# Attention weights turned unmasked and undivided, and the scaling moved behind the product with V

## Chip, cores and metric

The kernel runs on one core of one Trainium2 chip. The metric is the device time of one execution in microseconds. The kernel before takes 677.22 us, the median of three runs (677.18 to 677.5).

## The reference

An attention with a sliding window and four sink keys, followed by a feed-forward layer with a leaky maximum, all in float32:

```python
scores = (q @ k.T) / sqrt(D)                       # B,H,S,D = 4,8,768,64
keep = (pos[None] < 4) | ((rel >= 0) & (rel < 128))
scores = where(keep, scores, -1e9)
a = exp(scores - max(scores))
a = a / (sum(a) + 1e-9)
x = (a @ v), heads side by side                    # 3072 x 512
h = x @ w_in                                       # 512 -> 2048
out = (maximum(h, 0) + alpha * minimum(h, 0)) @ w_out
```

## The kernel before

The 3072 rows of x are 12 chunks of 256 queries (c; three chunks per batch, CPB). A chunk's feed-forward part is 16 slots (f, blocks of 128 of the 2048 columns). A slot is twelve matmuls of 128x256 for the first layer (L894: the high half of x by both halves of w_in, the low half by the high one), then ScalarE's multiplication by alpha (L898), VectorE's maximum (L899), ScalarE's rounded copy `gh` (L900) and VectorE's rest `gl` (L901), and, two slots later (LAG), six matmuls of 128x512 of the second layer (L931, L932, L929). First-layer results alternate between two PSUM banks.

While the matmuls of chunk c run, the attention of chunk c+1 is put between them, spread over twelve of the sixteen slots. Chunks 0 to 2 go other ways, which the change leaves alone. For chunks 3 to 11 (PAIRED) a head (h) and a half of its queries (u) is one step:

- SyncE (SP) loads `stage` (L443), VectorE and ScalarE split it into `kq` (L561 to L565).
- TensorE: two score matmuls of 128x260 (L597, L598): 256 window keys and 4 sinks.
- VectorE adds the mask and takes the row's extreme in one custom operation (L610), ScalarE takes the exponential with its sum (L614), both in a tile `pt_`. Masked weights come out as zeros.
- Then the head is finished. VectorE adds 1e-9 to the sums and takes reciprocals (L643, L644). A query's window covers at most the 128 keys before its block and the 128 of its own, and their two triangles don't overlap; so one custom operation (L655; L651 where a batch begins) adds the two blocks and divides, into `comb`. GpSimd divides the sink weights (L659).
- After two heads: VectorE turns 32x32 blocks of the pair's 512 columns (L741), SP writes the tile to DRAM (`swap`, L744) and reads it back in another order (L746), which makes it a full transpose. VectorE multiplies by two triangular masks to part the blocks again (L770 for pairs 0 and 1 into `wa`; L757 and L759 for pairs 2 and 3).
- The sinks of all heads are split, turned and sent through DRAM alike (L689, L690, L697, SP's `turns` L699 and `sinkT` L701).
- TensorE: four matmuls for the sinks (L859), and later 48 for the values (L786 for pairs 0 and 1, L875 for 2 and 3), 64 columns wide, two heads side by side. ScalarE and VectorE split the result into `xh` (L881) and `xl` (L882), the input of the next chunk's first layer.

The order is set ahead of time. Each operation is given to a planner (`Plan`) with its engine, an estimated cost, what it reads and writes, and for a DMA its bytes; the planner draws one queue for each engine, in which instructions then run strictly in order, and gives out the few buffers of each kind in turn. SP's DMAs go through one such queue too. What an instruction waits for can therefore hold all that stands behind it on its engine.

## Time and profile before

| | |
|---|---|
| time, median of three runs | 677.22 us (677.18 to 677.5) |
| span of the profiled execution | 676.2 us |
| TensorE busy | 663.8 us, 98% |
| VectorE busy | 525.8 us, 78% |
| ScalarE busy | 397.5 us, 59% |
| GpSimd busy | 34.5 us, 5% |
| bytes moved by DMAs | 85.19 MB |

The profile shows one execution; its span is 1.0 us under the median of the measured times. A row of a group reads: line, engine, operation, out<-in, shapes, count | busy us in all, mean ns of one | idle us ahead of them and what ended it. A row of the timeline reads: start in us, length, engine, line, operation. The length of a matmul includes the way through the array, so the pace is read from the distance of starts. Rows of waits read: us in total, times, the longest.

### The profile page before, as it was taken

Reading aid. Unit: us, or ns where it says so; the run is one execution under the profiler, and the core shown is the slowest. Engines: PE = TensorE matmul, PEld = TensorE weight load, DVE = VectorE, ACT = ScalarE, POOL = GpSimd, SP = SyncE. Lnnn points to the kernel's source line nnn. Section 1 sums busy time; section 2 is a strip of 40 time slices with the busy share of each in tenths; the row PEclk is TensorE's granted clock in tenths of the full one; section 3 lists DMA queues with packets and bytes.
Section 4 is the critical chain, followed back from the end, with each engine's and each line's share of the span. In section 5 each row is a group of like instructions: output and inputs, shape, how many; then the busy total and the mean of one; then the engine's idle time right before and its main releaser. Section 6 shows DMA issues by size and latency. Waiting matters only on the chain.

```text
span 676.2 us, 13243 instructions
## 1 busy us (share of the span) xinstructions
PE 663.8 (98%) x4532; PEld 580.5 (86%) x4534; DVE 525.8 (78%) x1750; ACT 397.5 (59%) x1066; POOL 34.5 (5%) x115
## 2 busy tenths in 40 slices
PE   9989999999999999999999999999999999999996
PEld 4577898888989989989988988988998988998995
DVE  6999999968967976986986995995895994994331
ACT  6989888827636726736636735644744753853332
POOL 2110000001000000000000000010000000000000
PEclk9979999999999999999999999999999999999999
DMA  8684641424343453443443433552542543420001
GB/s 314 229 277 151 241 187 39 127 71 147 122 133 107 122 148 93 145 132 95 141 118 114 143 107 93 163 140 61 172 128 78 161 128 88 142 94 17 32 2 35
DMA packets 58683, 85.19 MB, mean 126 GB/s; under 512 B 9072, under 2 KB 35056, under 8 KB 58608
## 3 DMA queue, kind: packets, MB, share of 16 engines
q1 hardware_dynamic: 55056, 71.17, 34.7%
q10 hardware_dynamic: 3552, 13.11, 5.4%
q8 instruction: 37, 0.61, 0.4%
q14 instruction: 38, 0.31, 0.1%
HBM read 67.22 MB, written 17.04 MB: 125 GB/s over the span
## 4 chain that ended last, share of the span: by engine, by line
PE 83%; DVE 9%; ACT 5%; issue 2%; POOL 0%; DMA 0%; ACTq 0%; SPq 0%; POOLq 0%
PE bank L894 35%; PE bank L931 12%; PE bank L932 11%; PE bank L929 11%; PE bank L786 3%; PE bank L598 3%; PE bank L597 3%; PE bank L875 2%; DVE wa L396 2%; ACT pt L614 1%; ACT wa L382 1%; DVE wa L394 1%; DVE w L404 1%; DVE g L899 1%; DVE gl L901 1%
## 5 line engine op out<-in xcount | busy, mean ns | idle before, releaser
L894 PE MATMUL bank<-xh,w 128*128 128x256 f32 x1536 | 307.9, 283 | 0.4 <-DVE g L899 0.2
L894 PEld LDWEIGHTS bank<-xh,w 128*128 128x128 f32 x1536 | 250.6, 189 | 9.0 <-DVE g L899 3.0
L894 PE MATMUL bank<-xl,w 128*128 128x256 f32 x768 | 215.1, 280 | 0.1
L898 ACT ACTIVATE g<-bank,param 128x256 f32<-128x256 f32 x192 | 90.5, 472 | 117.4 <-PE bank L894 113.1
L931 PE MATMUL bank<-w,gh 128*128 128x512 f32 x382 | 151.7, 397 | 0.2 <-ACT gh L900 0.2
L932 PE MATMUL bank<-w,gh 128*128 128x512 f32 x382 | 150.1, 393 | 0.0
L894 PEld LDWEIGHTS bank<-xl,w 128*128 128x128 f32 x768 | 145.2, 189 | 4.4 <-DVE xl L808 0.3
L614 ACT ACTIVATE pt<-pt,nm 128x260 f32<-128x260 f32 (+1 forms) x192 | 94.5, 493 | 53.5 <-DVE nm L610 53.1
L899 DVE TENSOR_TENSOR g<-bank,g 128x256 f32<-128x256 f32 x192 | 79.7, 419 | 51.4 <-ACT g L898 50.9
L929 PE MATMUL bank<-w,gl 128*128 128x512 f32 x382 | 119.5, 394 | 0.0
L900 ACT CAST gh<-g 128x256 fp32r<-128x256 f32 x192 | 76.9, 404 | 59.7 <-DVE g L899 59.6
L901 DVE TENSOR_TENSOR gl<-g,gh 128x256 fp32r<-128x256 f32 x192 | 80.5, 423 | 26.5 <-ACT gh L900 23.0
L610 DVE CUSTOM_DVE_ANT_0 pt<-bank,masks 128x260 f32<-128x260 f32 (+1 forms) x192 | 75.0, 401 | 19.3 <-PE bank L598 15.5
L929 PEld LDWEIGHTS bank<-w,gl 128*128 128x128 f32 x382 | 70.7, 188 | 16.2 <-issue 0.7
L931 PEld LDWEIGHTS bank<-w,gh 128*128 128x128 f32 x382 | 71.9, 188 | 9.5 <-ACT gh L900 0.7
L932 PEld LDWEIGHTS bank<-w,gh 128*128 128x128 f32 x382 | 71.9, 188 | 8.3
L563 DVE TENSOR_TENSOR kq<-stage,kq 64x392 fp32r<-64x392 f32 x80 | 45.3, 566 | 2.7
L659 POOL TENSOR_TENSOR sink<-pt,ri 128x8 f32<-128x8 f32 x80 | 20.8, 264 | 504.7 <-DVE ri L644 358.8
L597 PE MATMUL bank<-kq 128*128 128x260 f32 (+1 forms) x160 | 44.4, 278 | 1.3 <-DVE nm L610 1.3
L598 PE MATMUL bank<-kq 128*128 128x260 f32 (+1 forms) x160 | 45.0, 281 | 0.0
L655 DVE CUSTOM_DVE_ANT_0 comb<-pt,ri 128x128 f32<-128x128 f32 x136 | 43.1, 343 | 0.4
L561 ACT CAST kq<-stage 128x392 fp32r<-128x392 f32 x80 | 40.9, 512 | 0.7 <-ACT pt L614 0.2
(130 smaller groups left out, 686.9 us busy)
## 6 DMA issues: line engine op xcount, KB each, us to landing
stage<-qk SPq DMA_DIRECT2D x80, 324.0 KB, 2.9
wraw<-w ACTq DMA_DIRECT2D x12, 1024.0 KB, 5.9
swap<-comb SPq DMA_DIRECT2D x36, 256.0 KB, 2.0
comb<-swap SPq DMA_DIRECT2D x36, 256.0 KB, 3.2
v<-vq SPq DMA_DIRECT2D x36, 192.0 KB, 2.5
out_dram<-ob SPq DMA_DIRECT2D x22, 256.0 KB, 3.5
wraw<-w SPq DMA_DIRECT2D x4, 1024.0 KB, 12.0
v<-vp SPq DMA_DIRECT2D x8, 192.0 KB, 6.9
```

The source lines that it names most:

```text
L597: nc.tensor.matmul(s[:, w0], qh()[:, qs], ks()[:, kw], start=True, stop=False)
L598: nc.tensor.matmul(s[:, w0], ql()[:, qs], ks()[:, kw], start=False, stop=True)
L610: op("DVE", dve(n), lambda: nc.vector.tensor_tensor_reduce(out=pt.at[:, u, w0], in0=s.at[:, w0], in1=masks[:, i, w0], scale=-0.125, scalar ...
L614: op("ACT", exp(n), lambda: nc.scalar.activation(pt.at[:, u, w0], pt.at[:, u, w0], AF.Exp, bias=nm.at[:, h, u:u + 1], scale=-1.0, accum_ou ...
L894: nc.tensor.matmul(h(), fin.at[:, 0, part, ks], rhs.at[:, kt], start=(kt == 0 and n == 0), stop=(kt == KT - 1 and n == 2))
L898: op("ACT", act(QC, True), lambda: nc.scalar.activation(g.at, h(), AF.Copy, scale=alt[:, f:f + 1]), reads=[bk, known("param")], writes=[g])
L899: op("DVE", dve(QC), lambda: nc.vector.tensor_tensor(g.at, h(), g.at, ALU.max), reads=[bk], writes=[g])
L900: op("ACT", cast(QC), lambda: nc.scalar.copy(gh.at, g.at), reads=[g], writes=[gh])
L901: op("DVE", dve(QC), lambda: nc.vector.tensor_tensor(gl.at, g.at, gh.at.bitcast(F32), ALU.subtract), reads=[g, gh], writes=[gl])
L929: nc.tensor.matmul(o2[j].at, gl.at[:, js], fin.at[:, 1, 0], start=False, stop=(f == NF - 1))
L931: nc.tensor.matmul(o2[j].at, gh.at[:, js], fin.at[:, 1, 0], start=(f == 0), stop=False)
L932: nc.tensor.matmul(o2[j].at, gh.at[:, js], fin.at[:, 1, 1], start=False, stop=False)
```

## The change

For chunks 3 to 11 the weights stay as the exponential leaves them, with their zeros. For each head VectorE turns the 32x32 blocks of all four 128-wide pieces (two query halves, two key blocks) into half of a buffer `small`, of which there is one; after two heads SP moves it with four DMAs, each from 32 partitions of `small` to 128 partitions of a buffer `turn` (four of them), from SBUF to SBUF. There is no `swap` in DRAM, no merge and no mask multiplication, and GpSimd copies the sink weights undivided. The sums of a chunk get their 1e-9 and reciprocals once, are turned and written to DRAM (`sums`), and read back twice, each time broadcast to 64 partitions, into `scale`. The values' matmuls read `turn` in strides and follow the sinks' matmuls directly. VectorE then multiplies the PSUM result by `scale`; ScalarE and VectorE split the product from SBUF. `comb`, `wa`, `small` and three `turn` buffers lie in one tile, `room`; the first uses of it by chunk 3 wait for all users of `comb` and `wa`. Numbers of lines in the changed kernel differ: L902 is the first layer there, L939, L940 and L937 the second, L626 the mask, L907 and L909 the maximum and `gl`.

```diff
-    plan.kind("swap", [scratch.tile([4, P, P], F32, name=f"swap{i}") for i in range(2)])
+    plan.kind("sums", [scratch.tile([32, P], F32, name=f"sums{i}") for i in range(2)])
     plan.kind("turns", [scratch.tile([4, P, 2 * 32], F32, name=f"turns{i}") for i in range(2)])
-    trid = held(scratch.tile([P, 2, P], F32, name="trid"))
     several("stage", 2, [P, QC + KC], F32)
+    pts = [pool.tile([P, 2, WIN + NS], F32, name=f"pt_{i}") for i in range(3)]
     several("kq", 2, [P, KC + 2 * QC], F32R)
     several("v", 4, [P, 3, 2, D], F32)
-    several("pt_", 3, [P, 2, WIN], F32)
-    several("comb", 5, [P, 4 * P], F32)
-    several("wa", 2, [P, 2 * DM], I32)
+    room = pool.tile([P, 9 * DM], F32, name="room")
+    plan.kind("comb", [room[:, i * DM:(i + 1) * DM] for i in range(5)])
+    plan.kind("wa", [room[:, i * DM:(i + 2) * DM].bitcast(I32) for i in (5, 7)])
+    plan.kind("small", [room[:, 5 * DM:7 * DM]])
+    plan.kind("turn", [pool.tile([P, 2 * DM], F32, name="turn")] + [room[:, i * DM:(i + 2) * DM] for i in (7, 0, 2)])
+    several("scale", 1, [P, KT, QC], F32)
+    several("rs", 1, [P, 2, 32], F32)
+    plan.kind("pt_", [t[:, :, :WIN] for t in pts])
+    wholes = {id(at): t for (_, at), t in zip(plan.free["pt_"], pts)}
...
+        if c in SPLIT or c >= PAIRED:
+            op("POOL", 0.17, lambda: nc.gpsimd.tensor_copy(sk.at[:, :, h], pt.at[:, :, P:P + NS]), reads=[pt], writes=[(sk, h)])
+        if c >= PAIRED:
+            if h % 2 == 0:
+                turned[c, h // 2] = val("small")
+                if c == PAIRED and h == 0:
+                    late.append((turned[c, 0], ("comb", "wa")))
+            sl = turned[c, h // 2]
+            op("DVE", dve(4 * P), lambda: nc.vector.transpose(
+                sl.at.rearrange("p (j n t b) -> p n t j b", j=4, n=2, t=4)[:, h % 2],
+                whole(pt).rearrange("p u (m x) -> p (u m) x", m=2)[:, :, :P].rearrange("p t (j b) -> p t j b", j=4)), reads=[pt], writes=[(sl, h % 2)])
+            if h % 2:
+                swap(c, h // 2)
+            return
...
-        if c >= PAIRED and h % 2:
-            swap(c, h // 2)
...
-    def masks_in_order():
-        op("SP", ISSUE, lambda: nc.sync.dma_start(trid.at, tri), reads=[known("tri")], writes=[trid], nbytes=8 * P * P)
...
-        cb = comb.pop((c, p))
-        small, d, t = val("comb"), val("swap"), val("comb")
-        op("DVE", dve(4 * P), lambda: nc.vector.transpose(
-            small.at.rearrange("p (j t b) -> p t j b", t=4, j=4), cb.at.rearrange("p (t j b) -> p t j b", t=4, j=4)),
-            reads=[(cb, (j, u)) for j in range(2) for u in range(2)], writes=[small])
-        op("SP", ISSUE, lambda: nc.sync.dma_start(d.at.rearrange("i (a j) x -> (i a) (j x)", j=4), small.at),
-           reads=[small], writes=[d], nbytes=4 * P * 4 * P)
-        op("SP", ISSUE, lambda: nc.sync.dma_start(t.at.rearrange("p (i x) -> p i x", i=4), d.at.rearrange("i p x -> p i x")),
-           reads=[d], writes=[t], nbytes=4 * P * 4 * P)
-        turned[c, p] = t
-
-    def halved(c, p):
-
-        t, e = turned.pop((c, p)), val("comb")
-        at = lambda u: t.at.rearrange("p (i j u b) -> p u i j b", i=4, j=2, u=2)[:, u]
-        to = lambda u: e.at.rearrange("p (j u i b) -> p u i j b", i=4, j=2, u=2)[:, u]
-        mask = lambda l: tri[:, l].rearrange("p (i b) -> p i b", i=4).unsqueeze(2).broadcast_to([P, 4, 2, 32])
-        for u in range(2):
-            op("DVE", dve(2 * P), lambda u=u: nc.vector.tensor_tensor(to(u), at(u), mask(u), ALU.mult), reads=[t, known("tri")], writes=[(e, u)])
-        for u in range(2):
-            op("DVE", dve(2 * P), lambda u=u: nc.vector.tensor_tensor(at(u), at(u), mask(1 - u), ALU.mult), reads=[known("tri")], writes=[t])
-        wt[c, p] = (t, e)
-
-    def swapped(c, p):
-        if p > 1:
-            return halved(c, p)
-        t, tt = turned.pop((c, p)), val("wa")
-        full = lambda: tt.at.bitcast(F32).rearrange("p (j u l x) -> p j u l x", j=2, u=2, l=2)
-        view = lambda: t.at.rearrange("p (i j u b) -> p j u i b", i=4, j=2, u=2)
-        for j in range(2):
-            for u in range(2):
-                op("DVE", dve(2 * P), lambda j=j, u=u: nc.vector.tensor_tensor(
-                    full()[:, j, u].rearrange("p l (i b) -> p l i b", i=4),
-                    view()[:, j, u].unsqueeze(1).broadcast_to([P, 2, 4, 32]),
-                    tri.rearrange("p l (i b) -> p l i b", i=4), ALU.mult), reads=[t, known("tri")], writes=[(tt, (j, u))])
-        wt[c, p] = tt
+        sl, t = turned.pop((c, p)), val("turn")
+        if c == PAIRED:
+            late.append((t, ("comb", "wa")))
+        for i in range(4):
+            op("SP", ISSUE, lambda i=i: nc.sync.dma_start(
+                t.at[:, i * QC:(i + 1) * QC], sl.at[i * 32:(i + 1) * 32].rearrange("a (j x) -> a j x", j=4)),
+                reads=[sl], writes=[(t, i)], nbytes=4 * P * QC)
+        wt[c, p] = t
+
+    scales = {}
+
+    def inverse_sums(c):
+        sm, rs, d, r = sums[c], val("rs"), val("sums"), val("scale")
+        scales[c] = r
+        flat = lambda: rs.at[:, 0, :2 * H]
+        if c == PAIRED:
+            op("POOL", 0.15, lambda: nc.gpsimd.memset(rs.at, 0.0), writes=[rs])
+        op("DVE", 0.1, lambda: nc.vector.tensor_scalar(flat(), sm.at.rearrange("p h u -> p (h u)"), 1e-9, None, op0=ALU.add), reads=[sm], writes=[rs])
+        op("DVE", 0.1, lambda: nc.vector.reciprocal(flat(), flat()), writes=[rs])
+        op("DVE", 0.12, lambda: nc.vector.transpose(rs.at[:, 1], rs.at[:, 0]), writes=[rs])
+        op("SP", ISSUE, lambda: nc.sync.dma_start(d.at.rearrange("r (i x) -> i r x", i=4), rs.at[:, 1]),
+           reads=[rs], writes=[d], nbytes=4 * P * 32)
+        for n in range(2):
+            op("SP", ISSUE, lambda n=n: nc.sync.dma_start(
+                r.at[n * D:(n + 1) * D], d.at[:2 * H].rearrange("(p n u) x -> n p (u x)", n=2, u=2)[n:n + 1].broadcast_to([D, KT, QC])),
+                reads=[d], writes=[(r, 0), (r, 1)], nbytes=4 * D * KT * QC)
...
-        src = [*kept[:2], *kept[2], *kept[3]]
+        src, r = [wt.pop((c, x)) for x in every], scales.pop(c)
...
-                if x < 2:
-                    values(c, v[x].at, lambda j: kept[x].at.bitcast(F32)[:, j * 4 * P:(j + 1) * 4 * P], place(x), x == 1)
-                    continue
-                t, e = kept[x]
-                blocks = [(1, lambda j: t.at.rearrange("p (i j u b) -> p j u i b", i=4, j=2, u=2)[:, j], slice(0, 2 * P))]
+                turned_ = src[x].at.rearrange("p (i j n b) -> p j n i b", i=4, j=2, n=4)
+                blocks = [(1, slice(1, 3), slice(0, 2 * P))]
                 if c % CPB:
-                    blocks.append((0, lambda j: e.at[:, j * QC:j * QC + P], slice(0, P)))
-                blocks.append((2, lambda j: e.at[:, j * QC + P:(j + 1) * QC], slice(P, 2 * P)))
+                    blocks.append((0, 0, slice(0, P)))
+                blocks.append((2, 3, slice(P, 2 * P)))
                 for n, (blk, what, os) in enumerate(blocks):
                     for j in range(2):
-                        nc.tensor.matmul(place(x)[j * D:(j + 1) * D, os], v[x].at[:, blk, j], what(j), start=False, stop=x == KT - 1 and n == len(blocks) - 1)
+                        nc.tensor.matmul(place(x)[j * D:(j + 1) * D, os], v[x].at[:, blk, j], turned_[:, j, what], start=False, stop=x % 2 == 1 and n == len(blocks) - 1)
         op("PE", 4 * values_cost(c), all_values, reads=src + v, writes=bks, tail=N_TAIL, mode="col")
         for n, bk in enumerate(bks):
             part = slice(2 * n, 2 * n + 2)
             keys = [[(t, x) for x in range(2 * n, 2 * n + 2)] for t in (x1, x2)]
-            view = lambda bk=bk: bk.at.rearrange("p (n x) -> p n x", n=2)
-            op("ACT", cast(4 * P, True), lambda part=part, view=view: nc.scalar.copy(x1.at[:, part], view()), reads=[bk], writes=keys[0])
-            op("DVE", dve(4 * P), lambda part=part, view=view: nc.vector.tensor_tensor(x2.at[:, part], view(), x1.at[:, part].bitcast(F32), ALU.subtract),
-               reads=[bk, *keys[0]], writes=keys[1])
+            op("DVE", dve(4 * P), lambda part=part, bk=bk: nc.vector.tensor_tensor(
+                r.at[:, part], bk.at.rearrange("p (n x) -> p n x", n=2), r.at[:, part], ALU.mult), reads=[bk], writes=[(r, n)])
+            op("ACT", cast(4 * P), lambda part=part: nc.scalar.copy(x1.at[:, part], r.at[:, part]), reads=[(r, n)], writes=keys[0])
+            op("DVE", dve(4 * P), lambda part=part: nc.vector.tensor_tensor(x2.at[:, part], r.at[:, part], x1.at[:, part].bitcast(F32), ALU.subtract),
+               reads=[(r, n), *keys[0]], writes=keys[1])
...
-            steps += [lambda: trans(c, 2), sk, lambda: trans(c, 3), None, lambda: av_four(c)]
-            steps[10:10] = [lambda: trans(c, 0), lambda: trans(c, 1)]
-            return steps
+            return steps + [sk, lambda: inverse_sums(c), None, None, lambda: av_four(c)]
...
+    for v, names in late:
+        plan.after_all(v, plan.users(*names))
```

The planner draws new queues from this. TensorE's list is the same up to a place early in chunk 3's attention (at 165 us in the trace of before), and has as many matmuls in all. At the end of chunk 3's attention, TensorE's queue before, with the second layer of one slot, the sinks (L859) and the first layer of the next:

```order
L929 MATMUL bank_70<-w_917,gl_124 128x512
L929 MATMUL bank_71<-w_917,gl_124 128x512
L859 MATMUL bank_67<-sinkT_111,vs_112 128x256 x2
L859 MATMUL bank_66<-sinkT_111,vs_112 128x256 x2
L894 MATMUL bank_69<-xh_115,w_1071 128x256
L894 MATMUL bank_69<-xl_117,w_1071 128x256
```

and after, where the values (L882) are the next rows:

```order
L869 MATMUL bank_67<-sinkT_107,vs_108 128x256 x2
L869 MATMUL bank_66<-sinkT_107,vs_108 128x256 x2
L882 MATMUL bank_67<-turn,v_85 64x256 x2
L882 MATMUL bank_67<-turn,v_85 64x128 x2
L882 MATMUL bank_67<-room,v_86 64x256 x2
L882 MATMUL bank_67<-room,v_86 64x128 x2
L882 MATMUL bank_66<-room,v_87 64x256 x2
L882 MATMUL bank_66<-room,v_87 64x128 x2
L882 MATMUL bank_66<-room,v_88 64x256 x2
L882 MATMUL bank_66<-room,v_88 64x128 x2
L902 MATMUL bank_69<-xh_111,w_1067 128x256
```

Before, 21 matmuls of the first layer and six of the second stood between the sinks and the values; they now come behind the values.

SP's queue at the end of the next chunk's attention, chunk 4, before, with the last pairs' trips through DRAM and the sinks' (`turns`, `sinkT`):

```order
L746 DMA comb_91<-swap_75 128x4x128
L744 DMA swap_74<-comb_93 128x512
L746 DMA comb_90<-swap_74 128x4x128
L699 DMA turns_77<-pt_89 128x256
L744 DMA swap_75<-comb_94 128x512
L701 DMA sinkT_111<-turns_77 128x4x64
L746 DMA comb_93<-swap_75 128x4x128
L443 DMA stage_79<-qk 128x648
```

and after, with the DMAs from SBUF to SBUF (L764) and those of the inverse sums (L780, L783):

```order
L764 DMA room<-room 128x1x256 x3
L726 DMA turns_77<-pt_82 128x256
L764 DMA room<-room 128x1x256
L780 DMA sums_75<-rs_92 4x32x32
L459 DMA stage_79<-qk 128x648
L728 DMA sinkT_107<-turns_77 128x4x64
L783 DMA scale_91<-sums_75 64x4x256 x2
L474 DMA v_85<-vq 128x384
```

`sinkT` now stands behind the store of the sums and a load of `stage`, where one store to `swap` stood ahead of it.

VectorE's queue where a pair of heads follows another, late in chunk 5's attention, before (ISA is the custom operation of L610 and L655):

```order
L643 TENSOR_SCALAR ri_105<-sm_102 128x2 [waits Activation_49]
L901 TENSOR_TENSOR gl_124<-g_119,gh_121 128x256 [waits Activation_49]
L610 ISA pt_88,nm_100<-bank_64,masks 128x260 [waits PE_49,Pool_49]
L610 ISA nm_100 128x1
L644 RECIPROCAL ri_105<-ri_105 128x2 [waits DVE_49]
L655 ISA comb_90,jk_107<-pt_89,ri_104 128x128
L655 ISA jk_107 128x1
L741 STREAM_TRANSPOSE comb_93<-comb_90 128x4x4x32 [waits DVE_49]
L610 ISA pt_88,nm_100<-bank_65,masks 128x260 [waits PE_49]
L610 ISA nm_100 128x1
L899 TENSOR_TENSOR g_120<-bank_69,g_120 128x256 [waits Activation_49]
L770 TENSOR_TENSOR wa_95<-comb_92,tri 128x256 x2
```

and after (the names DMAHW with a number are the DMAs that a row waits for):

```order
L626 ISA pt_82,nm_96<-bank_65,masks 128x260 [waits PE_49]
L626 ISA nm_96 128x1
L579 TENSOR_TENSOR kq_84<-stage_79,kq_84 64x392 [waits DMAHW7_49,Activation_49]
L581 TENSOR_TENSOR kq_84<-stage_79,kq_84 128x256 [waits Activation_49]
L648 STREAM_TRANSPOSE room<-pt_81 128x4x4x32 [waits DMAHW2_49,DMAHW3_49,DMAHW1_49,DMAHW0_49]
L907 TENSOR_TENSOR g_116<-bank_69,g_116 128x256 [waits Activation_49]
L626 ISA pt_80,nm_96<-bank_64,masks 128x260 [waits PE_49,Pool_49]
L626 ISA nm_96 128x1
L648 STREAM_TRANSPOSE room<-pt_82 128x4x4x32
```

One transpose per head stands among the masks, and the first of a pair waits for the four DMAs of the pair before it, with a maximum (L907) and a mask (L626) behind it in the queue.

More of the change, by code (lines that the diff above doesn't have):

```diff
@@ L139, in op, with users, after_all @@
         return o
+    def users(self, *names):
+        return {o for o in self.ops if any(v.kind in names for v in o.values)}
+    def after_all(self, value, others):
+        for o in self.ops:
+            if value in o.values:
+                o.before.update(others)
     def order_after(self, o, *others):
@@ L365, in program @@
     raws, fins = {}, {}
+    late = []
+    whole = lambda v: wholes[id(v.at)]
     def load_weights(f, engine="ACT"):
@@ L694, in sink_step @@
             small, d = val("pt_"), val("turns")
-            flat = lambda: small.at.rearrange("p a x -> p (a x)")[:, :QC]
+            flat = lambda: whole(small).rearrange("p a x -> p (a x)")[:, :QC]
             st = sinkT[c] = val("sinkT")
@@ L719, in trans @@
             return
-        if c >= PAIRED:
-            return swapped(c, p)
         tp, cb, tt = val("pa"), comb.pop((c, p)), val("wa")
@@ L849, in av_four @@
         every = range(KT)
-        kept = [wt.pop((c, x)) for x in every]
-        src = [*kept[:2], *kept[2], *kept[3]]
+        src, r = [wt.pop((c, x)) for x in every], scales.pop(c)
         v = [vtile.pop((c, x)) for x in every]
@@ L951, in run @@
                 if u == 0:
-                    if h == 0 and c == PAIRED:
-                        masks_in_order()
                     if h == 0 and c and c % CPB == 0:
```

4 lines of the change are left out of this document (1 added, 3 removed).

## The prediction

> **What bounds the kernel now.** I began with the page: how busy each engine is over the whole span.
>
> ```profile
> span 676.2 us, 13243 instructions
> PE 663.8 (98%) x4532; PEld 580.5 (86%) x4534; DVE 525.8 (78%) x1750; ACT 397.5 (59%) x1066; POOL 34.5 (5%) x115
> ```
>
> TensorE (PE) is at 98% and VectorE (DVE) at 78%. A mean over stages doesn't say who waits, so I cut the span into windows: the start up to 165 us, the steady part, the last stores, then one chunk with attention in it and the last chunk, which has none. The columns are the length, then busy time (and instructions) of PE, weight load, DVE, ScalarE (ACT) and GpSimd (POOL), the granted clock, the DMA share and GB/s.
>
> ```profile
> 0.00:165.00 165.00, 158.43 (x1026) 126.12 (x1029) 146.72 (x396) 127.36 (x305) 14.42 (x44) 0.98 0.53 181
> 165.00:668.00 503.00, 502.82 (x3498) 452.62 (x3497) 378.70 (x1354) 268.96 (x760) 20.11 (x71) 1.00 0.37 109
> 668.00:676.20 8.20, 2.60 (x12) 1.76 (x10) 0.36 (x1) 1.17 (x2) 0.00 (x0) 0.92 0.21 72
> 247.40:300.20 52.80, 52.80 (x375) 47.52 (x374) 42.16 (x152) 29.49 (x84) 3.23 (x9) 1.00 0.43 127
> 614.80:668.00 53.20, 53.20 (x367) 47.66 (x367) 16.57 (x40) 18.00 (x40) 0.00 (x0) 1.00 0.03 11
> ```
>
> From 165 to 668 us PE is idle for 503.00 - 502.82 = 0.18 us. DVE has 42.16 us of work in a chunk of 52.80 us, 80%, and PE doesn't wait for it. The last chunk, with 16.57 us on DVE, is no shorter. The list of waits says the same: PE's whole account of waiting is seven lines, of which these are the largest:
>
> ```profile
> PE bank L588 <- DVE nm L610: 1.7, 2, 1.2
> PE bank L597 <- DVE nm L610: 1.3, 3, 0.8
> PE bank L1086 <- DVE fm L544: 1.0, 1, 1.0
> ```
>
> Since only 0.18 us of PE's idle time lies behind 165 us, nearly all of these 4.0 us lie ahead of it. The order of PE's instructions is the same in both kernels up to 165 us, early in chunk 3's attention, so I leave them where they are. What bounds the kernel is the number of matmuls and the pace at which PE runs them, and the change leaves the number alone.
>
> **The pace.** A busy PE isn't one pace. In the chain, each row is the twelve first-layer matmuls of one slot (start, length); their starts, in the last chunk, which has no attention beside it, give the length of a slot:
>
> ```profile
> 623.14 1.39 PE bank L894 x12
> ...
> 639.78 1.39 PE bank L894 x12
> 642.54 1.39 PE bank L894 x12
> 645.41 1.42 PE bank L894 x12
> 648.22 1.41 PE bank L894 x12
> ```
>
> The slot from 639.78 is 2.76 us, that from 645.41 is 2.81 us, with the same work and a clock of 1.00 (the window's row); the first-layer matmuls take 1.39 us before and 1.41 to 1.42 after. In between lies one longer slot, 2.87 us. What toggles it I can't read from the trace. It is the one property of the bounding engine that a new order could touch.
>
> **VectorE's relief.** These are the groups that chunks 3 to 11 lose (x36 is four a chunk, x72 eight), and two of the nearest kin to what they get:
>
> ```profile
> L655 DVE CUSTOM_DVE_ANT_0 comb<-pt,ri 128x128 f32<-128x128 f32 x136 | 43.1, 343 | 0.4
> L655 DVE DVE_READ_ACCUMULATOR2_ANT jk<- 128x1 f32 x136 | 11.4, 84 | 0.0
> L651 DVE TENSOR_SCALAR comb<-pt,ri 128x128 f32<-128x128 f32 x24 | 6.5, 273 | 0.2
> L643 DVE TENSOR_SCALAR ri<-sm 128x2 f32<-128x2 f32 x80 | 13.2, 166 | 1.0
> L741 DVE STREAM_TRANSPOSE comb<-comb 128x512 f32<-128x512 f32 x36 | 25.6, 711 | 1.0
> L770 DVE TENSOR_TENSOR wa<-comb,tri 128x256 f32<-128x256 f32 x72 | 27.2, 406 | 0.0
> L757 DVE TENSOR_TENSOR comb<-comb,tri 128x256 f32<-128x256 f32 x36 | 14.7, 449 | 0.1
> L759 DVE TENSOR_TENSOR comb<-comb,tri 128x256 f32<-128x256 f32 x36 | 13.6, 420 | 0.0
> L837 DVE TENSOR_TENSOR ob<-bank,ob 128x512 f32<-128x512 f32 x4 | 2.7, 684 | 0.0
> L882 DVE TENSOR_TENSOR xl<-bank,xh 128x512 fp32r<-128x512 f32 x18 | 12.5, 692 | 26.0 <-ACT xh L881 26.0
> L881 ACT CAST xh<-bank 128x512 fp32r<-128x512 f32 x18 | 10.5, 586 | 25.5 <-PE bank L786 16.4 <-PE bank L875 9.0
> ```
>
> Removed per chunk: the dividing merges (43.1 + 11.4 + 6.5)/10 = 6.1 us (these groups and the next one serve ten chunks, 2 to 11); the sums' +1e-9 and, at the same price, the reciprocals 2 x 13.2/10 = 2.6; transposes 25.6/9 = 2.8; mask multiplies (27.2 + 14.7 + 13.6)/9 = 6.2. Together 17.7 us. Added: eight transposes of 512 at 711 ns = 5.7, two products PSUM x scale at L837's 684 ns = 1.4, and three small ones at L643's 166 ns = 0.5: 7.6 us. DVE falls by 10.1 us a chunk, from 42.2 to about 32, over nine chunks by 91 us. On the path this is worth nothing, by the windows: 0.18 us of idle PE is all there is to gain.
>
> **Values behind the sinks.** PE's rows at the end of a chunk's attention, and the chain that leads to them, from the timeline (start, length):
>
> ```profile
> 232.92 0.28 PE L598 MATMUL bank<-kq 128*128 128x260 f32 x1
> 233.84 0.52 ACT L614 ACTIVATE pt<-pt,nm 128x260 f32<-128x260 f32 x1
> 236.48 0.45 DVE L697 STREAM_TRANSPOSE pt<-ts 128x256 f32<-128x256 f32 x1
> 239.18 0.38 SPq L701 DMA_DIRECT2D sinkT<-turns  x1
> 242.97 0.63 PE L859 MATMUL bank<-sinkT,vs 128*128 128x256 f32 x4
> 247.39 1.96 PE L786 MATMUL bank<-wa,v 128*64 128x256 f32 x24
> 249.18 1.91 PE L875 MATMUL bank<-comb,v 128*64 128x256 f32 x24
> 251.02 0.39 PE L894 MATMUL bank<-xh,w 128*128 128x256 f32 x1
> swap<-comb SPq DMA_DIRECT2D x36, 256.0 KB, 2.0
> comb<-swap SPq DMA_DIRECT2D x36, 256.0 KB, 3.2
> turns<-pt SPq DMA_DIRECT2D x9, 128.0 KB, 1.7
> sinkT<-turns SPq DMA_DIRECT2D x9, 128.0 KB, 2.5
> v<-vp SPq DMA_DIRECT2D x8, 192.0 KB, 6.9
> ```
>
> (The last five rows are DMA issues: count, KB each, median us to landing.) The values take 249.18 - 247.39 = 1.79 us when they read `wa` in order and 251.02 - 249.18 = 1.84 us when they read `comb` in strides, which all of them now do: 0.05 us a chunk, 0.5 us over nine, if that difference is of the reading at all; I take 0 and keep +0.5 as the upper bound. They move from 247.39 to right behind L859, at about 243.6. There they need the last turned weights. The last exponential ends at 233.84 + 0.52 = 234.4; with DVE's queue the last transpose ends about 236, the fourth DMA goes out by 237.5 (four issues of 0.38 us), and lands 1.7 to 3.2 us later, 239.2 to 240.7. Slack: 3 to 4 us. Price 0.
>
> Behind them three slots of first-layer matmuls, 8.3 us, are left to the chunk's end instead of 15 matmuls. The new chain there is DVE product 0.68, ACT cast 0.59, DVE subtraction 0.69, twice, partly overlapped: 4 us at most. It also needs the inverse sums: out after DVE's three small operations, at about 237.5, landing 2.0 us later, read back in another 3.2 us, with SP's queue about 244; the values end at 243.6 + 3.6 = 247.2. Price 0.
>
> **SP's queue.** `sinkT` now stands behind the store of the sums and a `stage` load that waits for DVE (L581, behind the three small operations). Before, `sinkT` was issued at 239.18, landed 2.5 us later at 241.7, and PE took it at 242.97: 1.3 us to spare. Now DVE is less loaded and the sinks' copies (GpSimd) need no reciprocal, so the first transfer goes out about 0.5 us earlier; the sums' issue and the load's wait give about that back. I take 1.3 us to spare again, price 0; bounds: nothing, or each us of lateness beyond 1.3 paid nine times.
>
> **The one buffer `small`.** The first transpose of a pair waits until the four DMAs of the pair before have read `small`; on DVE a mask (L626) and an activation's maximum (L907) are queued behind it, and PE waits for both through its banks. Room: eight heads over twelve slots of 52.8/16 = 3.3 us are 4.95 us a head, less a transpose of 0.71: 4.2 us. Need: three issues of 0.38 us ahead of the last, 1.1 us, and then 1.7 us (`turns`, from SBUF, 128 KB like these) to 2.5 us (`sinkT`): 2.8 to 3.6 us. It fits by 0.6 to 1.4 us. And a late DVE isn't a late PE at once: second-layer matmuls run two slots behind, and the two banks of the first layer allow somewhat under a slot, about 2 us. Price 0; the upper bound is among the rivals, the lower bound is 0, as nothing waits less on PE.
>
> A rule speaks against these DMAs. The Trainium skill, SBUF — State Buffer, "Door 1: The DMA port swizzle", says that 32 partitions reach 8 of 16 ports and so half the bandwidth, and its section "The DMA setup-cost knee" gives about 2 us fixed plus the bytes at up to 436 GB/s, and asks for all partitions and one large transfer. The change does the contrary: four transfers, each read from 32 partitions. By that, an estimate from that page, one takes 2 + 0.13/0.218 = 2.6 us and the group 3.7 us, which still fits in 4.2. `turns`, 128 KB from 128 partitions, at 1.7 us shows a smaller fixed cost than the page's; no run here shows 32 partitions.
>
> **Sum.** 676.2 us profiled, 0 for each part: 676.2. The measured times have a median of 677.22, 1.0 above the span; I add that: **677.2 us**.
>
> **Rivals.** About 0.2% of the time, 1.35 us, is what a measurement of this kernel tells from no change; "same" is 675.9 to 678.6.
>
> *The pace shifts, faster.* In the last chunk the slow pace holds from 645.41 to the end at 668, about half of the time since 623.14, at 0.05 us a slot. The steady part has 503/3.3 = 152 slots; if half of them are slow too (an estimate from that chunk), all fast would bring 76 x 0.05 = 3.8 us. Half of that, 1.9 us, gives 675.3 us. For it: DVE and ACT touch less memory beside PE. Against it: the last chunk, almost free of DVE work and DMAs, has both paces. Chance 0.20.
>
> *The pace shifts, slower.* The same to the other side, 679.1 us. The scores move to other places among PE's matmuls, which can turn it either way. Chance 0.16.
>
> *`small` comes free late (slower).* It decides where a group of four DMAs takes over 4.2 + 2 = 6.2 us, as the `v<-vp` row with 6.9 us would. Then 0.7 us is lost at three hand-offs in each of nine chunks: 27 x 0.7 = 19 us, 696 us; at half that excess 687 us. Against it: `v<-vp` belongs to the start with a DMA share of 0.53, here it is 0.43, and the rows of 128 KB in the steady part, `turns` and `sinkT`, are at 1.7 and 2.5 us. Chance 0.06.
>
> *`sinkT` late behind SP's queue (slower).* If the `stage` load's wait for DVE lasts 1.3 us longer than I put it plus 1 us, nine times 1 us: 686 us. Chance 0.04.
>
> *The change doesn't do what it says.* The number of matmuls is the same, and the transposes still run on DVE; if DVE fell by much less than 10 us the time would be the same. This lies inside my forecast.
>
> **Numbers.** The forecast has 0.54. Range: downwards two thirds of the 3.8 us, 677.2 - 2.6 = 674.6; upwards half of them and the 0.5 us of strided reading, 677.2 + 1.9 + 0.5 = 679.6. With the forecast the two cases of the pace hold about 0.88 of the chance inside it; the 0.10 of late transfers are left out above. Faster 0.20, same 0.54, slower 0.26.
>
> **What would show it.** In the trace of after: PE idle under 0.5 us between 165 and 668 us; DVE near 32 us in a chunk's window of 52.8; the values right behind L869 without a wait; no PE wait for a mask (L626) or for `sinkT`; the groups of four landing within 3.6 us. The prediction is wrong if PE shows recurring waits, above all for L626's banks, or if the starts of slots differ by much more than 0.05 us from before.

## The result, and the profile after

The changed kernel takes 702.11 us, median of four runs (700.09 to 709.7), where the kernel before takes 677.36 beside it: 1.0385 times as long (95% interval 1.0331 to 1.0439). The forecast was 677.2 us, with a range from 674.6 to 679.6. The profiled execution has a span of 698.4 us, 22.2 more than before.

The page first, then TensorE's list of waits:

```profile
span 698.4 us, 12956 instructions
PE 671.4 (96%) x4534; PEld 584.1 (84%) x4534; DVE 460.8 (66%) x1279; ACT 401.3 (57%) x1066; POOL 37.8 (5%) x116
```

```profile
PE bank L869 <- DMA sinkT<-turns: 13.2, 9, 2.8
PE bank L604 <- DVE nm L626: 2.2, 2, 1.2
PE bank L613 <- DVE nm L626: 1.8, 3, 0.9
```

VectorE is relieved, by 65 us on the page. A new line stands at the top of the waits, though: in each of the nine chunks the sinks' matmuls (L869) wait for `sinkT`, 13.2 us together. The waits for masks (L604, L613) are 1.0 us longer than before, 4.0 in place of 3.0.

The windows show what else there is: the steady part, the wait at the end of chunk 4's attention, and the values behind it in two pieces (columns as before, the granted clock third from the end).

```profile
165.00:690.00 525.00, 510.89 (x3495) 456.49 (x3494) 314.31 (x893) 272.39 (x760) 23.44 (x71) 0.99 0.42 113
...
243.20:246.20 3.00, 0.41 (x2) 0.00 (x0) 0.46 (x2) 0.41 (x1) 0.00 (x0) 1.00 0.77 190
247.00:249.00 2.00, 2.00 (x15) 1.59 (x16) 0.00 (x0) 0.00 (x0) 0.00 (x0) 0.50 0.53 121
249.00:252.20 3.20, 3.20 (x38) 2.34 (x35) 0.69 (x1) 0.62 (x1) 0.00 (x0) 0.81 0.37 105
```

Behind the wait TensorE runs at half its clock: the trace shows a granted clock of 0.50 from 246.8 to 250.2 us. The timeline of the same place, VectorE, SyncE's queue and TensorE:

```profile
230.00 3.50 SPq L764 DMA_DIRECT2D room<-room  x4
235.85 0.71 DVE L648 STREAM_TRANSPOSE room<-pt 128x512 f32<-128x512 f32 x1 [2.52 <-DMA room<-room]
236.49 0.39 DVE L626 CUSTOM_DVE_ANT_0 pt<-bank,masks 128x260 f32<-128x260 f32 x1
...
238.60 1.84 SPq L764 DMA_DIRECT2D room<-room  x3
238.80 0.21 DVE L716 CAST ts<-sink 128x128 fp32r<-128x128 f32 x1
239.37 0.45 DVE L724 STREAM_TRANSPOSE pt<-ts 128x256 f32<-128x256 f32 x1
240.53 0.54 SPq L726 DMA_DIRECT2D turns<-pt  x1
241.75 0.59 SPq L780 DMA_DIRECT2D sums<-rs  x1
242.98 0.38 SPq L728 DMA_DIRECT2D sinkT<-turns  x1
246.28 0.82 PE L869 MATMUL bank<-sinkT,vs 128*128 128x256 f32 x4 [2.67 <-DMA sinkT<-turns]
247.03 1.97 PE L882 MATMUL bank<-turn,v 128*64 128x256 f32 x12
248.79 3.47 PE L882 MATMUL bank<-room,v 128*64 128x256 f32 x36
252.19 0.38 PE L902 MATMUL bank<-xh,w 128*128 128x256 f32 x1
```

Read from the top: four DMAs go out from 230.00; the first transpose of the next pair (L648) waits 2.52 us for them; behind it on VectorE stands the mask (L626) of the last scores, which TensorE had started at 233.5; it starts at 236.49. The exponential, the sinks' small operations, `turns` and `sinkT` all follow that mask. `sinkT` goes out when `turns` has landed, 2.45 us after its issue, and lands 3.25 us later. Then the values take 252.19 - 247.03 = 5.16 us in place of 3.63.

VectorE's own list has the waits for `small`, 20.5 us in 20 waits:

```profile
DVE room L648 <- DMA room<-room: 13.5, 11, 2.5
DVE room L648 <- DMA turn<-room: 7.0, 9, 2.0
```

In this chunk the sinks' turn (L724) ends 6.3 us behind the last scores, against 4.0 in the kernel before: 2.3 us later. `turns` then goes out 0.7 us behind it, as three of the last pair's DMAs are issued first; `sinkT` goes out 0.2 us later behind `turns` than before and lands 0.7 us later. Together that is 3.9 us of lateness; less the 1.3 us to spare, it gives the wait of 2.67 us but for rounding.

The DMAs' rows: count, KB, median us to landing.

```profile
room<-room SPq DMA_DIRECT2D x108, 128.0 KB, 2.7
...
turn<-room SPq DMA_DIRECT2D x36, 128.0 KB, 2.8
...
turns<-pt SPq DMA_DIRECT2D x9, 128.0 KB, 2.4
sinkT<-turns SPq DMA_DIRECT2D x9, 128.0 KB, 2.9
```

In six chunks the last mask is 2.2 to 3.0 us behind its scores; in the three whose batch begins it is on time, and their sinks wait 0.2 to 0.9 us only. Of the 22.2 us, 13.2 are the waits, 3.2 the slow values in two chunks (5.16 and 5.30 us against 3.62 each), 1.0 the waits for masks. Some 2.5 us lie around the nine waits: in chunk 4, from the last second-layer matmul to the first of the values to start it is 3.82 us, against 0.80 in the kernel with both mends, below, which has no wait: 3.02 us for a listed wait of 2.67. The nine such differences, 0.35 at most, sum to 2.5 us. About 1.7 us more is a slower pace of TensorE, which the kernel with both mends shows by itself.

### The profile page after: what moved, and what is told of

It is laid out like the page before. It is cut to its first block, busy times and chain, and to the rows that moved or that the text cites. A ratio compares the mean times of both kernels' runs of the same rounds, so it can differ in the third digit from the quotient of the medians.

```text
span 698.4 us, 12956 instructions
## 1 busy us (share of the span) xinstructions
PE 671.4 (96%) x4534; PEld 584.1 (84%) x4534; DVE 460.8 (66%) x1279; ACT 401.3 (57%) x1066; POOL 37.8 (5%) x116
## 4 chain that ended last, share of the span: by engine, by line
PE 53%; DMA 15%; DVE 14%; ACT 8%; issue 5%; SPq 4%; POOL 1%; ACTq 0%; DVEq 0%; POOLq 0%
PE bank L902 22%; PE bank L939 7%; PE bank L937 7%; PE bank L940 7%; DMA room<-room 5%; PE bank L882 5%; SPq L764 4%; DMA sinkT<-turns 4%; DVE room L648 3%; DMA turns<-pt 3%; ACT pt L630 3%; DVE pt L626 2%; DMA turn<-room 2%; DVE gl L909 2%; DVE g L907 1%
## 5 line engine op out<-in xcount | busy, mean ns | idle before, releaser
L902 PE MATMUL bank<-xh,w 128*128 128x256 f32 x1536 | 307.4, 282 | 0.2
L902 PEld LDWEIGHTS bank<-xh,w 128*128 128x128 f32 x1536 | 249.5, 188 | 7.2 <-issue 1.5
L902 PE MATMUL bank<-xl,w 128*128 128x256 f32 x768 | 215.1, 280 | 0.1
L939 PE MATMUL bank<-w,gh 128*128 128x512 f32 x382 | 151.8, 398 | 0.2 <-ACT gh L908 0.2
L940 PE MATMUL bank<-w,gh 128*128 128x512 f32 x382 | 151.1, 395 | 0.0
L902 PEld LDWEIGHTS bank<-xl,w 128*128 128x128 f32 x768 | 144.8, 189 | 4.6 <-DVE xl L819 0.3
L907 DVE TENSOR_TENSOR g<-bank,g 128x256 f32<-128x256 f32 x192 | 80.2, 418 | 86.7 <-ACT g L906 86.3
L937 PE MATMUL bank<-w,gl 128*128 128x512 f32 x382 | 120.3, 396 | 0.0
L909 DVE TENSOR_TENSOR gl<-g,gh 128x256 fp32r<-128x256 f32 x192 | 79.1, 413 | 40.3 <-ACT gh L908 39.5
L626 DVE CUSTOM_DVE_ANT_0 pt<-bank,masks 128x260 f32<-128x260 f32 (+1 forms) x192 | 75.3, 399 | 19.5 <-PE bank L614 16.1
L937 PEld LDWEIGHTS bank<-w,gl 128*128 128x128 f32 x382 | 70.7, 188 | 16.5 <-issue 0.3
L939 PEld LDWEIGHTS bank<-w,gh 128*128 128x128 f32 x382 | 71.8, 188 | 9.7 <-ACT gh L908 0.6
L940 PEld LDWEIGHTS bank<-w,gh 128*128 128x128 f32 x382 | 71.8, 188 | 8.8
L648 DVE STREAM_TRANSPOSE room<-pt 128x512 f32<-128x512 f32 x72 | 50.7, 707 | 20.7 <-DMA room<-room 13.5
L641 POOL COPY sink<-pt 128x8 f32<-128x8 f32 x88 | 28.6, 329 | 489.1 <-ACT pt L630 479.4
L613 PE MATMUL bank<-kq 128*128 128x260 f32 (+1 forms) x160 | 44.7, 279 | 1.9 <-DVE nm L626 1.8
```

Source lines behind the costliest of these rows:

```text
L626: op("DVE", dve(n), lambda: nc.vector.tensor_tensor_reduce(out=pt.at[:, u, w0], in0=s.at[:, w0], in1=masks[:, i, w0], scale=-0.125, scalar ...
L648: op("DVE", dve(4 * P), lambda: nc.vector.transpose(sl.at.rearrange("p (j n t b) -> p n t j b", j=4, n=2, t=4)[:, h % 2], whole(pt).rearra ...
L902: nc.tensor.matmul(h(), fin.at[:, 0, part, ks], rhs.at[:, kt], start=(kt == 0 and n == 0), stop=(kt == KT - 1 and n == 2))
L907: op("DVE", dve(QC), lambda: nc.vector.tensor_tensor(g.at, h(), g.at, ALU.max), reads=[bk], writes=[g])
L909: op("DVE", dve(QC), lambda: nc.vector.tensor_tensor(gl.at, g.at, gh.at.bitcast(F32), ALU.subtract), reads=[g, gh], writes=[gl])
L937: nc.tensor.matmul(o2[j].at, gl.at[:, js], fin.at[:, 1, 0], start=False, stop=(f == NF - 1))
```

## The experiments

Theory A: the wait for `small` delays VectorE's queue, with it the last mask, and through the sinks' chain, which had 1.3 us to spare, TensorE; a slower clock follows long waits. Rival B: SyncE's queue, where the sums' store and a load stand ahead of `sinkT`. Rival C: a slower pace of TensorE all over.

**Two buffers `small`.**

```diff
-    room = pool.tile([P, 9 * DM], F32, name="room")
+    room = pool.tile([P, 11 * DM], F32, name="room")
-    plan.kind("small", [room[:, 5 * DM:7 * DM]])
+    plan.kind("small", [room[:, i * DM:(i + 2) * DM] for i in (5, 9)])
-    nc = _bacc.Bacc("TRN2", target_bir_lowering=False, num_devices=1, dynamic_dma_scratch_size=8192)
+    nc = _bacc.Bacc("TRN2", target_bir_lowering=False, num_devices=1, dynamic_dma_scratch_size=4096)
```

> The changed kernel with two buffers for small, so that the first transpose of a pair need not wait for the four DMAs of the pair before it. Theory A (the wait for small delays the last masks by 2.2 to 2.6 us in six of nine chunks, and through the sinks' chain the matmuls of L869): the last mask starts within 0.5 us of its scores in those chunks too, L869 waits 0.3 to 1.0 us in each chunk (13.2 us before, about 5 after), no stretch runs at half clock, and the time falls from about 702 to 683 to 688 us. Rival B (SyncE's queue: the sums' store and the stage load ahead of sinkT): no change of L869's wait, 698 to 704 us. Rival C (a slower pace of TensorE all over): no change, about 700 us.

684.57 us, 1.0112 times before (1.0078 to 1.0146). Its waits, and the last masks of chunk 4:

```profile
PE bank L869 <- DMA sinkT<-turns: 4.1, 5, 1.5
...
PE bank L613 <- DVE nm L626: 0.9, 2, 0.8
```

```profile
234.05 0.43 DVE L626 CUSTOM_DVE_ANT_0 pt<-bank,masks 128x260 f32<-128x260 f32 x1 [0.81 <-PE bank L614]
...
235.44 0.71 DVE L648 STREAM_TRANSPOSE room<-pt 128x512 f32<-128x512 f32 x1
```

The mask now waits for its scores, starts 0.33 us behind them in every chunk, and all values take 3.62 or 2.75 us. A holds: 17.5 us of the loss by the medians, 14.4 by the profiled executions, hang on the one buffer. (The smaller scratch for DMAs, which makes room for the second buffer, wasn't tried alone; two kernels below mend the wait without it.) The 4.1 us left come from five chunks, so even then the margin is gone: VectorE has the sinks' turn done 3.7 us behind the last scores (4.0 in the kernel before), but SyncE issues `turns` at 4.4 in most chunks (4.0 in the kernel before), behind the DMAs of the last pair.

**The sums' step moved back.**

```diff
-            return steps + [sk, lambda: inverse_sums(c), None, None, lambda: av_four(c)]
+            return steps + [sk, None, None, lambda: inverse_sums(c), lambda: av_four(c)]
```

> The changed kernel with the inverse sums' step moved behind two empty steps, so that the sums' store is planned later. Theory A: sinkT is issued as soon as its turns have landed, whatever stands ahead of it; L869 waits 11 to 14 us in all and the time stays at 698 to 706 us. Rival B: with the store of the sums behind sinkT, each L869 waits 0.6 to 1.5 us less, and the time falls to 688 to 694 us.

699.43 us, 1.0318 times (1.0277 to 1.0359). The planner left the store of the sums where it was, between `turns` and `sinkT`, so this run tells nothing of B. It shows the clock once more: in this profile the values behind distances of 3.28 and 2.42 us (from the start of the last matmul ahead of the wait to the first behind it) took 6.02 and 5.30 us, behind one of 2.88 us the usual 3.62.

**The sums behind `sinkT`.** The same question, with the order forced: the planner holds the store of the sums until `sinkT`.

```diff
-            op("SP", ISSUE, lambda: nc.sync.dma_start(st.at.bitcast(F32).rearrange("p (i x) -> p i x", i=4), d.at.rearrange("i p x -> p i x")),
+            last_sink[c] = op("SP", ISSUE, lambda: nc.sync.dma_start(st.at.bitcast(F32).rearrange("p (i x) -> p i x", i=4), d.at.rearrange("i p x -> p i x")),
...
-        op("SP", ISSUE, lambda: nc.sync.dma_start(d.at.rearrange("r (i x) -> i r x", i=4), rs.at[:, 1]),
+        o = op("SP", ISSUE, lambda: nc.sync.dma_start(d.at.rearrange("r (i x) -> i r x", i=4), rs.at[:, 1]),
...
+        plan.order_after(o, last_sink[c])
```

> The changed kernel with the store of the inverse sums behind sinkT in SyncE's queue (the run with the step moved left it ahead of sinkT, so it told nothing of the queue). Theory A: sinkT goes out when turns has landed, 2.4 to 2.5 us after its issue, whatever stands between; it may go out 0.1 to 0.3 us sooner, L869 waits 11 to 14 us in all, 697 to 704 us. Rival B (the sums' store and the load held sinkT up): 0.6 us or more off each of nine waits, 688 to 694 us.

694.70 us, 1.0252 times (1.0235 to 1.0269): between what A and B gave. The chain of waits of this kernel, and of the changed one:

```profile
241.83 2.45 DMA turns<-pt
244.30 2.76 DMA sinkT<-turns
298.54 2.42 DMA turns<-pt
301.03 2.77 DMA sinkT<-turns
```

```profile
240.53 2.43 DMA turns<-pt
242.98 3.25 DMA sinkT<-turns
...
300.52 3.51 DMA sinkT<-turns
```

`sinkT` goes out 2.47 us after `turns` in this kernel and 2.45 in the changed one, so the queue didn't hold it, against B. But it lands 0.5 to 0.7 us sooner in these two chunks, which I had not expected. In the others, by TensorE's start behind the issue, the gain is 0 to 0.4 us. The sums' small transfer is no longer just ahead; as the load of `stage` also goes out earlier, mostly by 0.7 us, the run doesn't part the two. The waits fall from 13.2 us:

```profile
PE bank L870 <- DMA sinkT<-turns: 9.8, 8, 2.2
```

In this profile the values of three chunks run slow (5.30 us), behind distances of 2.09, 2.27 and 2.61 us; behind one of 2.12 they don't.

**A slot later.** The sinks' and the values' matmuls from the 156th to the 168th first-layer matmul of a chunk.

```diff
+        if c + 1 < NCHUNK and c + 1 >= PAIRED:
+            work[-NF + SPAN - 1 + 2].append(work[-NF + SPAN - 1].pop())
```

> The changed kernel with the sinks' and the values' matmuls one slot later (from the 156th to the 168th first-layer matmul of a chunk), all else as it was. Theory A: the lateness of sinkT, 1 to 3 us, is covered by the slot of 2.8 us; L869 waits under 1 us in all, no half clock, 677 to 681 us, if the scaling still ends before the next chunk begins with 24 first-layer matmuls left; if it doesn't, the first matmul of a chunk waits for xh instead, some tenths of a us each. Rival C (pace): 690 us or more.

679.94 us, 1.0050 (1.0030 to 1.0070). The wait that is left:

```profile
PE bank L869 <- DMA sinkT<-turns: 0.3, 1, 0.3
```

The last masks are as late as ever (1.8 to 3.1 us in the same six chunks); one slot covers them. So the lateness of `sinkT` is nearly all of the loss, and the new chain behind the values fits in two slots.

**Costs told to the planner.** One buffer, but the four DMAs get their measured issue and a later landing.

```diff
-            op("SP", ISSUE, lambda i=i: nc.sync.dma_start(
+            op("SP", 0.65, lambda i=i: nc.sync.dma_start(
...
-                reads=[sl], writes=[(t, i)], nbytes=4 * P * QC)
+                reads=[sl], writes=[(t, i)], nbytes=4 * P * QC, tail=1.2)
```

> The changed kernel with the planner told that one of the four DMAs takes 0.65 us to issue and lands 1.2 us later than it thinks; it then puts the last masks and the sinks' chain ahead of the transposes that wait for small. One buffer small, as before. Theory A: the masks are on time, turns go out 1.5 to 2.5 us sooner, L869's waits fall from 13.2 to 0 to 4 us, 677 to 684 us; the values may then wait for turn instead, which are later. Rival B: no change of L869's wait, near 700 us.

680.61 us, 1.0044 (1.0027 to 1.0061). The largest waits of TensorE are again those that lie ahead of the change, and L869 is in no line:

```profile
PE bank L604 <- DVE nm L626: 2.2, 2, 1.2
PE bank L1090 <- DVE fm L560: 1.0, 1, 1.0
```

There is still one buffer, but no transpose waits for it any more. The masks and the sinks' operations stand ahead of the last pair's transposes, which start with no idle time before them:

```profile
238.80 0.45 DVE L724 STREAM_TRANSPOSE pt<-ts 128x256 f32<-128x256 f32 x1
239.16 1.26 DVE L648 STREAM_TRANSPOSE room<-pt 128x512 f32<-128x512 f32 x2
```

The first transpose of a pair now comes 5.1 us or more behind the last one before it, where the changed kernel left 3.4 us in six chunks. So one buffer costs little in itself; what costs is urgent work queued behind a wait for it. The planner also put `turns` ahead of the last pair's DMAs, 3.4 us behind the last scores, so this run doesn't part VectorE's share from SyncE's.

**Half of the issues on ScalarE.**

```diff
-            op("SP", ISSUE, lambda i=i: nc.sync.dma_start(
+            op("ACT" if i % 2 else "SP", ISSUE, lambda i=i: (nc.scalar if i % 2 else nc.sync).dma_start(
```

> The changed kernel with every second one of the DMAs from small to turn issued by ScalarE in place of SyncE. Theory A: the last of a group goes out about 0.6 us after the first in place of 1.9 us, so small comes free about 1.3 us sooner; the last masks are late by about 1 us in place of 2.2 to 2.6, L869 waits 4 to 8 us in all (13.2 before), 684 to 692 us. If it is the landing and not the issues that makes the group slow, the waits and the time stay near 700 us.

695.11 us, 1.0264 (1.0227 to 1.0301): a miss by 3 us. Its DMAs:

```profile
room<-room SPq DMA_DIRECT2D x54, 128.0 KB, 3.0
room<-room ACTq DMA_DIRECT2D x54, 128.0 KB, 3.4
...
turns<-pt SPq DMA_DIRECT2D x9, 128.0 KB, 3.8
```

`small` does come free sooner: VectorE's waits for it fall from 20.5 to 6.7 us, and the last masks of the six chunks are only 0.3 to 1.7 us behind their scores. But landings get longer, 3.0 to 3.7 us in place of 2.7 and 2.8, and `turns`, among them in the queue, takes 3.8 in place of 2.4. `sinkT` goes out 3.2 to 4.5 us behind `turns` in place of 2.5, and TensorE still waits 10.5 us for it. The Trainium skill, DMA: Bandwidth & Descriptors, "Rules for kernel authors", says that spreading DMAs over issuing engines saves only issue time, as all run on the same DMA engines; the landings here agree.

**Whole partitions.** Each of the four DMAs reads 128 partitions of a quarter of `small` in place of 32 partitions of all of it. The weights aren't exchanged between partitions then, so the values are of other weights.

```diff
-                t.at[:, i * QC:(i + 1) * QC], sl.at[i * 32:(i + 1) * 32].rearrange("a (j x) -> a j x", j=4)),
+                t.at[:, i * QC:(i + 1) * QC], sl.at[:, i * QC:(i + 1) * QC]),
```

> The changed kernel with each of the four DMAs of a pair reading 128 partitions of a quarter of small (1 KB each) in place of all of 32 partitions: the same bytes to the same places in the same order, but the blocks aren't exchanged, so the values get wrongly turned weights. Theory A with the 32-partition reads as the cause of the slow groups: an issue takes 0.33 us in place of 0.60, the group lands within 3.5 us of the second transpose in place of 4.7, L869 waits 3 to 6 us, 682 to 688 us. If reads of 32 partitions aren't what is slow, issues stay at 0.60 us and the time near 700 us.

684.16 us, 1.0108 (1.0091 to 1.0124).

```profile
room<-room SPq DMA_DIRECT2D x108, 128.0 KB, 2.1
...
turn<-room SPq DMA_DIRECT2D x36, 128.0 KB, 2.2
turns<-pt SPq DMA_DIRECT2D x9, 128.0 KB, 2.0
```

Half right: the landing falls from 2.7 to 2.1 us, and with it the waits for `sinkT` to 2.5 us; an issue stays at 0.59 us. So 32 partitions cost 0.6 us of landing, and the long issue has another cause. The time is theory A's.

**Half the bytes, half the pieces.** Two looks at the issue, with half of `turn` left zero: 512 B of each row, or 16 of the 32 partitions.

```diff
+                t.at[:, i * QC:i * QC + P], sl.at[i * 32:(i + 1) * 32].rearrange("a (j x) -> a j x", j=4)[:, :, :P]),
```

> The changed kernel with each DMA from small to turn moving 512 B of each of its 128 rows in place of 1 KB (the other half of turn stays zero, so the values get half of the weights): as many pieces, half the bytes. If the issue of 0.60 us goes by the number of pieces it stays at 0.60 us; if by the bytes it falls to about 0.35 us. The landing, 2.7 us, falls to about 2.3 us if the bytes through the ports of 32 partitions make it long. The time falls to 683 to 692 us as the group lands sooner.

```diff
+                t.at[:64, i * QC:(i + 1) * QC], sl.at[i * 32:i * 32 + 16].rearrange("a (j x) -> a j x", j=4)),
```

> The changed kernel with each DMA from small to turn reading 16 of its 32 partitions and writing 64 in place of 128 (the other half of turn stays zero, so the values get half of the weights): half the pieces and half the bytes. If the issue goes by pieces it falls to about 0.35 us here and not in the run with half rows; if by bytes, in both; if by neither, in none. Theory A: 680 to 690 us where the group's end, issue and landing together, comes 1 us sooner.

680.89 and 686.74 us, one run each beside 678.38. Landings fall to 2.1 and 2.4 us:

```profile
room<-room SPq DMA_DIRECT2D x108, 64.0 KB, 2.1
```

```profile
room<-room SPq DMA_DIRECT2D x108, 64.0 KB, 2.4
```

The issue stays at 0.59 to 0.60 us in both, so it goes neither by the bytes nor by the pieces nor by the partitions that are read. What sets it is open. (With half rows a DMA needs only the pair's first transpose and goes out earlier, so that kernel's time can't be put to the bytes alone.)

**Idle matmuls in the wait.**

```diff
         def sinks():
+            for _ in range(6):
+                nc.tensor.matmul(bks[0].at, idle[:, :1].broadcast_to([P, P]), idle[:, 1:].broadcast_to([P, 512]), start=True, stop=True)
```

> The changed kernel with six idle matmuls of 128x512 (about 0.23 us each, 1.4 us) directly ahead of the sinks' matmuls in each of the nine chunks, so that TensorE works through half of the wait for sinkT. Theory A (the wait is in part followed by a lower clock): the values take 3.6 us in every chunk of two batches' inner blocks, none 5.2; that takes 3.2 us off the profiled run, and the idle matmuls add about 2 us in the chunks whose wait was shorter than they are: 696 to 700 us, with less spread than the changed kernel's 700 to 710. If the clock has another cause, 700 to 712 us.

700.51 us (698.86 to 701.44). TensorE's waits for `sinkT` fall to 4.9 us, no distance between two of its starts at these waits is over 1.9 us, and in its profile every chunk's values take 3.62 or 2.75 us. The runs lie within 2.6 us, where the changed kernel's spread over 9.6. The median is 0.5 over what I expected. The idle matmuls may cost about what the clock gives back; no run parts the two.

**Both mends.** Two buffers `small` and a slot later.

> The changed kernel with two buffers small and the sinks' and values' matmuls a slot later: both mends together. Theory A: no wait of L869 at all, 677 to 680 us, within 0.4% of the kernel before; TensorE is the bound again, so VectorE's 10 us a chunk bring nothing and it is not faster than before by more than 0.2%.

679.53 us, 1.0035 (1.0022 to 1.0047), and the steady part:

```profile
165.00:668.00 503.00, 503.00 (x3486) 453.11 (x3485) 318.33 (x892) 275.45 (x756) 19.79 (x71) 1.00 0.43 118
```

TensorE is busy for all of 503.00 us, VectorE for 318.33 where it was 378.70, and nothing is faster. No kernel beat the one before. This one is 2.4 us slower than before with no wait. Over eight whole chunks, from the 577th to the 2113th first-layer matmul and with the same matmuls in both, it takes 421.7 us against 420.1; TensorE is idle for 0.00 us in it and for 0.18 in the kernel before, and neighbouring second-layer matmuls start 233.1 ns apart on the mean, 231.7 before. So some 1.6 us is a slower pace, rival C at a small size. What sets the pace, and what the rest of the 2.4 us is, stays open.

## Why the prediction was wrong

**What held.** The bound: with the waits mended, TensorE is as full as before, and 60 us less on VectorE in that window are worth nothing. The relief was sized well: I had summed durations to 91 us less; the sum of all durations on VectorE falls by 103 us, of which the page's busy time, where operations overlap, shows 65. The pace mattered little: it is slower by 1.6 us over eight chunks in the kernel with both mends, whose 679.53 us come near the 679.1 of the prediction's slower pace. Rival C, with 0.36 of the chance in its two forms, explains no more than that of the 22 us.

**The step that failed: `small`.** "Need: three issues of 0.38 us ahead of the last, 1.1 us, and then 1.7 us ... to 2.5 us ...: 2.8 to 3.6 us. It fits by 0.6 to 1.4 us." Both sides of this comparison were wrong. The need: the fourth issue started 1.9 us behind the first (0.60 each; 2.9 in chunk 4, where the third was held up) and the landing took 2.7 us, so that in the six chunks with a late mask the next transpose started 4.8 to 5.9 us behind the last one of the pair before. The room: 4.2 us is a mean over a chunk, but at the last pair of these chunks VectorE was free after 3.4 us (4.1 to 5.9 at the other pairs within a chunk). The differences are the waits there, 1.4 to 2.5 us. I had priced the issues from DMAs of another kind (0.38 us) and the landing from rows of 128 partitions. My estimate by a rule of the Trainium skill (SBUF — State Buffer, "Door 1: The DMA port swizzle") was 2.6 us for one transfer from 32 partitions, and the runs agree: 2.7 us from 32 partitions, 2.1 from 128. I held `turns` with 1.7 us against it, although that differs in this point, and in going to DRAM.

**The step behind it: who waits.** "A late DVE isn't a late PE at once ... about 2 us." I had looked at TensorE's banks, and there it is right: 1.0 us more of waits for masks. But behind the waiting transpose stood the last mask of a chunk, and behind that a chain of fixed length to `sinkT` with 1.3 us to spare. I had both numbers, the room of the wait and the margin of the chain, in two paragraphs and never added them: 2.2 to 3.0 us late on a margin of 1.3.

**The margin itself.** "I take 1.3 us to spare again." Without the wait for `small` five chunks still lose 4.1 us: `turns` leaves 0.4 us later in most chunks and lands after 2.5 in place of 1.7 us, `sinkT` after 2.9 in place of 2.5. In the changed kernel `turns` stands behind the last pair's DMAs for 0.7 us or more in every chunk, a cost that I had put at nothing.

**The rivals.** "`small` comes free late" had the cause (0.06), and put it on the wrong path, at 19 us for a group of 6.9 us; it was to decide from 6.2 us, and groups that took 4.8 us were enough. "`sinkT` late behind SP's queue" (0.04) had the place and a price of 9 us, and in the main the wrong cause: SyncE's queue gave 0.7 us, ahead of `turns` and not of `sinkT`. Neither had the clock, which makes a wait of 2.7 us cost 1.5 us more.

## What to carry to other kernels

Where a change adds a wait, follow what is queued behind the waiting instruction to the end of its chain, not only to the next buffer, and subtract the lateness from the margin found there. Compare what a buffer needs with the room at the tightest place, not with a mean. Price transfers by rows with the same partitions, the same two ends and the same neighbours in the queue. A shared buffer need not be doubled if the planner knows the true times and puts the urgent work ahead of what needs the buffer.

## What the runs showed of the hardware

- TensorE's clock fell to half behind distances of 2.1 to 3.5 us between the starts of two matmuls, and not behind all of them: in the changed kernel behind 3.07 and 3.22 us, in two others not behind 2.88 and 2.12 us, but behind 2.42 and 2.09. It followed no wait for `sinkT` with a distance under 2.09 us in any of the profiled executions. The Trainium skill, TensorE: Matmul & The Clock Gate, "What's actually happening", puts the fall behind an idle window of about 3.4 us that runs freely; that the outcome varies fits a free window, its length doesn't fit distances of 2.1 to 3.3 us. With six idle matmuls in the gap the distances stayed under 1.9 us, the clock held, and four runs spread over 2.6 us in place of 9.6.
- A DMA from 32 partitions to 128 in SBUF landed after 2.7 us, one of the same 128 KB from 128 partitions after 2.1 us.
- Issues of such DMAs on SyncE took 0.60 us each, single ones up to 1.9 us. Those of SBUF to DRAM took 0.33 us in the kernel before (`swap`, `turns`), and 0.54 us for `turns` right behind such DMAs in the changed one.
